# Half of the gate and value weights narrowed inside batch 0, one projection unit per block

## The chip, the cores and the metric

One core of a Trainium2 chip runs the whole program. The metric is the device time of one execution in microseconds (us). TensorE does the matmuls (PE; its weight loads are PEld), VectorE is DVE, ScalarE is ACT, GpSimd is POOL, and SyncE (SP) issues the transfers. Each engine runs its own instructions in the order in which they were put into its queue, and waits on semaphores for the other engines.

## The reference

```
p_packed = attention(p, k, v)              # 8 batches x 8 heads, 32 packed rows, 576 keys, width 64
x = attention(q, p_packed, p_packed)       # 8 x 8 heads, 576 queries against the 32 packed rows
x = x.transpose(0, 2, 1, 3).reshape(4608, 512)
xn = x / sqrt(mean(x*x) + 1e-6) * rms_g
x = (silu(xn @ w_gate) * (xn @ w_val)) @ w_out     # 512 -> 1536 -> 512
h = x @ w_in                                       # 512 -> 2048
out = (h * cos(h)) @ w_out2                        # 2048 -> 512
```

q, k, v, p and rms_g arrive as 32-bit floats. The five weight matrices arrive as 64-bit floats; the kernel makes 32-bit floats of them on the chip, which it calls narrowing.

## The kernel before

**Arithmetic.** A 32-bit product is made of three matmuls of fp32r operands (`mm3`, L143): each operand is split into a high part (ACT, L106) and the rest, the low part, a subtraction (DVE or POOL, L107). `hilo` (L105) does both; its argument `eng` chooses the engine of the low part.

**Narrowing** (`narrow`, L122). A chunk of 128 partitions x 512 numbers (512 KB of doubles) takes five steps, each waiting for the one before: an absolute value on ACT (L129), a maximum with a tiny number (L130, on POOL or DVE), a shift (L133), and two merges (L136, L139) on DVE. `w_gate` and `w_val` make 24 chunks (their tiles are `wraw`, narrowed into `wy`), `w_out` 12 (narrowed into `ny`, then split into `wohl`).

**Packed attention stage** (L489 to L523). 16 steps, two a batch: load keys (`kn`), values (`vn`) and `p`, transpose the keys, form scores (their maximum is L381, once a step), exponentials, and the packed rows. Steps 3 to 15 also load and narrow the 24 chunks and the first four of `w_out`, 28 in all, by `w_due` (L482), and from step 3 on do the first 26 pieces of the query attention of batch 0 (`attend`, L209). In this stage the order on each engine is chosen by a planner of the framework.

**Projection** (`project`, L555). Everything from L718 on stands in the order in which the code emits it. Instead of multiplying x by the gate and value weights, the kernel multiplies the packed rows by them once, and applies the attention weights to the product. There are 24 units; unit n needs chunk n. A unit splits the chunk of the next unit (`pj_stack`, L546: two high parts on ACT, one low part on DVE and one on POOL, tiles `stk`), does 16 matmuls, copies four PSUM tiles (`mps`) out into two `ev` tiles (two copies on ACT, two on DVE), and sends them to DRAM by six transfers (`m0raw` four, `m` two). There are four `ev` tiles. `pj_to` (L708) runs units up to a number: eight before batch 0, then two in each of its blocks 0 to 7, one ahead of the block's matmuls and one behind.

**Blocks** (L774 on). A batch is 24 blocks, of two halves of the tokens and 12 slices of 128 of the hidden width. Block i does `gv_block` (12 matmuls, `gv`; a sigmoid on ACT L655, two products on DVE, L656 and L657, tile `silu`), a piece of the next batch's query attention (`att_step`), `split_s` (L660: high part on ACT, low part on DVE, tile `shl`), and `acc_block` of block i-2 (12 matmuls, `acc`). gv, the projection and the attention share four PSUM tiles (`ps_gv`). Behind that come the jobs of the table at L772 to L836: load, narrow and split a slice of `w_out` (`WO_AT`: load at, narrow at, split one block later), split the gate and value product of a coming pair of slices (`wm_split`, `SPLIT0`), load a product of batch 1 (`M0_AT`), reload partial sums (`X1_AT`). In batch 0 the low parts of `wm_split` are on DVE (`WM0_POOL`), in the other batches on POOL. `after_project` (L697) frees the projection's memory and opens the pools of the later loads; until then `w_out` slices are loaded into `ev` tiles (slices 4 and 5).

Of the kernel before, what the change touches and what calls it, by code (L numbers as in the profile page):

```python
# [9 lines left out]
F32 = mybir.dt.float32  # L10
# [10 lines left out]
def kernel(  # L21
# [22 lines left out]
    HALF = S // 2  # L44
# [3 lines left out]
    NCK = FF1 // 256  # L48
# [14 lines left out]
    WRAW_B = 3  # L63
    WO_U = 4
    SEG, M0_D = 6, 0
    W_FROM, W_TO, W_POOL = 3, 16, 3
    ATT_U, U_ATT, U_ATT_N = 26, 3, 2
    PJ_0, PJ_F, PJ_L = 8, 2, 0
    STT_M, STT_P = 4, 0
    STK_M, STK_P, STK_B, EV_B = 1, 3, 2, 4  # L70
    EV_DVE = (1, 3, 5, 7)
    WM0_POOL = False
    W2_I0, W2_AT, W2_POOL = 25, (1, 3, 5, 7, 14, 18), False
    T_END, F3_B = 2, 3
    LAG, LAG_B = 2, 3
    WO_AT = {4: (0, 2), 5: (2, 4), 6: (7, 9), 7: (8, 10), 8: (9, 11), 9: (10, 12), 10: (12, 14), 11: (13, 16)}
    M0_AT, M_AT = (9, 10, 11, 12, 13, 14), (3, 5, 7, 9, 11, 14)
    ATT_ORD = "t00 t01 x00 x01 x02 x03 t10 r00 t11 s00 x10 x11 p00 x12 p01 x13 - r10 - s10 - p10 p11"
    ATT_ORD0 = "t00 t01 x00 x01 x02 x03 r00 s00 p00 p01 t10 t11 x10 x11 x12 x13 r10 s10 p10 p11"
    AL_AT = 16  # L80
    X1_AT = (14, 20)
    ATT_FROM, ATT_TO, ATT_FROM0, N_ATT = 0, 48, 0, 43
    WM_O, M_I0 = 0, 11
    BX, BS, BW = 0, 3, 6
# [24 lines left out]
    def load_w(pool, tag, src, bufs=None):  # L109
        r, f = src.shape  # L110
        j = r // 128
        shape = [128, j, f, 2] if wide else [128, j, f]
        t = pool.tile(shape, I32 if wide else F32, tag=tag, name=tag, bufs=bufs)
        if wide:
            nc.sync.dma_start(
                out=t.rearrange("p j f t -> p j (f t)"), in_=src.bitcast(I32).rearrange("(j p) f -> p j f", p=128)
            )
        else:
            nc.sync.dma_start(out=t, in_=src.rearrange("(j p) f -> p j f", p=128))
        return t  # L120

    def narrow(raw, y, pool=True):  # L122

        if not wide:
            nc.vector.tensor_copy(y, raw)
            return
        yi = y.bitcast(I32)
        up, low = raw[:, :, :, 1], raw[:, :, :, 0]
        nc.scalar.activation(out=y, in_=raw.bitcast(F32)[:, :, :, 1], func=AF.Abs)  # L129
        (nc.gpsimd if pool else nc.vector).tensor_scalar(  # L130
            out=y, in0=y, scalar1=TINY_HI, scalar2=None, op0=ALU.max
        )
        nc.vector.tensor_scalar(  # L133
            out=yi, in0=yi, scalar1=3, scalar2=0x3FFFFFFF, op0=ALU.logical_shift_left, op1=ALU.bitwise_and
        )
        nc.vector.scalar_tensor_tensor(  # L136
            out=yi, in0=up, scalar=-0x40000000, in1=yi, op0=ALU.bitwise_and, op1=ALU.bitwise_or
        )
        nc.vector.scalar_tensor_tensor(  # L139
            out=yi, in0=low, scalar=29, in1=yi, op0=ALU.logical_shift_right, op1=ALU.bitwise_or  # L140
        )
# [296 lines left out]
    w_y = {}  # L438

    def w_load(n):  # L440
        if n >= 4 * NCK:
            wo_load(n - 4 * NCK, u3, "wraw")
            return
        i, a = divmod(n, 2)
        c, gv = divmod(i, 2)
        w = w_val if gv else w_gate
        w_raw[n] = load_w(u3, "wraw", w[a * 256:(a + 1) * 256, c * 256:(c + 1) * 256], WRAW_B)

    def w_prep(n):
        if n >= 4 * NCK:  # L450
            wo_prep(n - 4 * NCK, u3)
            return
        i, a = divmod(n, 2)
        c, gv = divmod(i, 2)
        if a == 0:
            w_y[i] = wm_p.tile([128, 4, 256], F32, tag="wm", name="wy")
        narrow(w_raw.pop(n), w_y[i][:, 2 * a:2 * a + 2], n % W_POOL == W_POOL - 1)

    att_done = [0]
    late = {}  # L460
# [4 lines left out]
    def wo_load(f, pool, tag):  # L465
        wo_raw[f] = load_w(pool, tag, w_out[f * 128:(f + 1) * 128, :], {"wraw": WRAW_B, "ev": EV_B}.get(tag))

    def wo_prep(f, pool):
        y = pool.tile([128, 1, DM], F32, tag="ny", name="ny", bufs=2 if "w2" in late else 1)
        narrow(wo_raw.pop(f), y, False)  # L470
        wo_y[f] = y
        if f < WO_U:
            wo_split(f)
# [3 lines left out]
        o = wo_t[f] = wo_p[f >= WO_U].tile([128, 2, DM], F32R, tag="wo", name="wohl")  # L477
        hilo(y[:, 0], o[:, 0], o[:, 1], nc.gpsimd if f >= WO_U else None)

    n_w = 4 * NCK + WO_U  # L480

    def w_due(i):  # L482
        a, b = (n_w * max(0, min(x, W_TO) - W_FROM) // (W_TO - W_FROM) for x in (i, i + 1))
# [180 lines left out]
    def acc_block(b, hf, f):  # L664
        n = NF1 if b else SEG
        if f % n == 0:
            acc_t[b, hf] = [ps_acc.tile([128, HALF], F32, tag="acc", name="acc") for _ in range(KD)]
        sh = s_t.pop((b, hf, f))
        wo = wo_t[f]
        for d in range(KD):  # L670
            mm3(
                acc_t[b, hf][d], wo[:, 0, d * 128:(d + 1) * 128], wo[:, 1, d * 128:(d + 1) * 128],
                sh[:, 0], sh[:, 1], f % n == 0, f % n == n - 1,
            )
        if f % n == n - 1:
            c0 = b * S + hf * HALF
            for d2 in range(2):
                x1_at = x1_dram[:, 2 * d2:2 * d2 + 2, c0:c0 + HALF]
                x1 = x1_t.pop((b, hf, d2), None)
                if x1 is None:  # L680
                    x1 = late.get("x", f1).tile([128, 2, HALF], F32, tag="x1", name="x1")
                if f >= n:
                    for r in range(2):
                        nc.vector.tensor_tensor(out=x1[:, r], in0=acc_t[b, hf][2 * d2 + r], in1=x1[:, r], op=ALU.add)
                else:
                    nc.vector.tensor_copy(x1[:, 0], acc_t[b, hf][2 * d2])
                    nc.scalar.activation(out=x1[:, 1], in_=acc_t[b, hf][2 * d2 + 1], func=AF.Copy)  # L687
                nc.sync.dma_start(out=x1_at, in_=x1)

    x1_t = {}  # L690

    def x1_load(hf):
        for d2 in range(2):
# [75 lines left out]

    wm_next = [(b, c) for b in range(1, B) for c in range(NCK)] + [("w", x) for x in range(NCK)]  # L770
    B1 = 2 * NF1
    SPLIT0 = (-1, 1, 3, 5, 7, 9, 13, 14, 16, 19, 21, 23)  # L772
    wm_split()
    for i in range(len(seq) + LAG):  # L774
        b, hf, f = seq[min(i, len(seq) - 1)]
        j = i % B1
        if i < len(seq):
            if j == 0:
                if att is not None:
                    for _ in att:  # L780
                        pass
                att = attend(b + 1) if b + 1 < B else None
                att_done[0] = 0
                if b == B - 1:
                    ast.close()
                    rst.close()
                    bx["p"] = ctx.enter_context(tc.tile_pool(name="bx", bufs=2, side="right", reuse_waits="tile"))
            if b == 0:
                pj_to(PJ_0 + PJ_F * i + 1)
            t = gv_block(b, hf, f)  # L790
            att_step(2 * i)
            split_s(b, hf, f, t)
            if b == 0:
                pj_to(PJ_0 + PJ_F * (i + 1))
                if pj_n[0] == 4 * NCK and not late:
                    after_project()
        if i >= LAG:
            acc_block(*seq[i - LAG])
            att_step(2 * i + 1)
            b, hf, f = seq[i - LAG]  # L800
            if (b, hf) == (B - 1, 0):
                if f == BX:
                    load_x(0)
                if f in (BS, BS + 2):
                    split_x(0, (f - BS) // 2)
                if f >= BW and f < BW + 4:
                    w2_split(f - BW + NF1)
                if f >= BW - 2 and f < BW + 2:
                    w2_load(f - BW + 2 + NF1)
                if f >= NF1 - 2:  # L810
                    w2_load(f - NF1 + 2)
            if (b, hf) == (B - 1, 1):
                w2_split(f)
                if f + 2 < NF1:
                    w2_load(f + 2)
            b, hf, f = seq[min(i, len(seq) - 1)]
        for n, (at, to) in WO_AT.items():
            if at == i:
                wo_load(n, *((late["w2"], "raw") if late else (pr_p, "ev")))
            if to == i:  # L820
                wo_prep(n, late.get("w2", f1))
            if to + 1 == i:
                wo_split(n)
        if i in X1_AT:
            x1_load(X1_AT.index(i))
        if j == AL_AT and b < B - 2:
            att_load(b + 2)
        if i in SPLIT0 if i <= SPLIT0[-1] else b < B - 1 and hf == 1 and f % 2 == 1:
            wm_split()
        if i < len(seq) and b == B - 1 and j >= 11 and j % 2:  # L830
            if j < 23:
                wm_load(wm_next.pop(0))
            if j > 11:
                wm_split()
        if b < B - 1 and j in (M_AT if b else M0_AT):
            wm_load(wm_next.pop(0))  # L836
        if i >= W2_I0 and j in W2_AT:
            w2_fetch()
            w2_narrow(len(w2_items) > 0)
# [112 lines left out]
```

## Time and profile before

| what | value |
|---|---|
| median of 3 runs | 1806.87 us (1806.51 to 1807.89) |
| profiled execution | 1800.86 us |
| its span, first to last instruction | 1799.1 us |
| PE busy | 1701.4 us, 95% of the span |
| DVE busy | 1151.8 us, 64% |
| ACT busy | 921.0 us, 51% |
| POOL busy | 216.0 us, 12% |
| mean granted clock of TensorE | 0.983 |

Busy times are those of the profiled execution, and its own time is 1800.86 us, 1.76 us more than the span. The median of the runs without a profile is 6.0 us above it. A share of the whole span says little here, since the stages differ: the packed attention stage lies from 0 to about 172 us, eight projection units to 215.67 us, batch 0 (its first gv matmul to that of batch 1) from 215.67 to 382.18 us, batch 1 from 382.18 to 472.70 us. The granted clock is the share of TensorE's full clock; it has two levels, 1.2 and 2.4 GHz, so a value between is a mean of both.

### The profile page before, as it was taken

How to read it: one execution, taken by the hardware profiler on the slowest of the kernel's cores; microseconds unless marked ns; L12 is line 12 of the kernel's file. 1: busy time of each engine (PE TensorE's matmuls, PEld its weight loads, DVE VectorE, ACT ScalarE, POOL GpSimd, SP SyncE). 2: the span in 40 equal slices, each digit the busy share in tenths (PEclk: the TensorE clock that was granted, in tenths of full speed). 3: DMA queues.
4: the chain of work that ended last, by engine and by line, in shares of the span. 5: the costliest groups of instructions: out<-in, count | busy, mean ns of one | idle time of the engine just before them, and what ended most of it. 6: DMA issues, size and time to landing. Idle time of an engine off the chain costs nothing.

```text
span 1799.1 us, 26917 instructions
## 1 busy us (share of the span) xinstructions
PE 1701.4 (95%) x10144; PEld 1526.2 (85%) x10144; DVE 1151.8 (64%) x2212; ACT 921.0 (51%) x1773; POOL 216.0 (12%) x186
## 2 busy tenths in 40 slices
PE   7878678799999999999999999999999999999998
PEld 5766568699999999999999788888888888888887
DVE  4677567867676767676756756565656566555554
ACT  4767556445444444454444645454545555454444
POOL 2111222321212121212121300000000000000000
PEclk9989889899999999999999999999999999999999
DMA  9993677434343424242213301010101010100000
GB/s 253 250 255 112 199 210 221 142 108 133 98 135 96 137 94 139 92 143 90 90 61 113 125 1 48 0 48 0 48 0 48 1 47 15 33 1 24 1 24 24
DMA packets 117802, 164.55 MB, mean 91 GB/s; under 512 B 26792, under 2 KB 82088, under 8 KB 117672
## 3 DMA queue, kind: packets, MB, share of 16 engines
q1 hardware_dynamic: 117672, 162.83, 30.7%
q8 instruction: 79, 1.29, 0.3%
q14 instruction: 51, 0.42, 0.1%
HBM read 107.61 MB, written 52.04 MB: 89 GB/s over the span
## 4 chain that ended last, share of the span: by engine, by line
PE 77%; DVE 5%; ACT 3%; DMA 2%; issue 1%; SPq 1%; POOL 0%; DVEq 0%; ACTq 0%
PE ops L146 7%; PE ops L144 7%; PE ops L145 7%; PE hp L144 7%; PE hp L145 7%; PE hp L146 7%; PE gv L144 5%; PE acc L144 5%; PE acc L145 5%; PE acc L146 5%; PE gv L145 5%; PE gv L146 5%; PE sp L227 1%; DMA m<-ev 1%; PE qtp L217 1%
## 5 line engine op out<-in xcount | busy, mean ns | idle before, releaser
L144 PE MATMUL gv<-apt,wmhl 128*128 128x288 f32 x768 | 235.5, 307 | 34.2 <-DVE silu L656 20.1
L144 PE MATMUL acc<-shl,wohl 128*128 128x288 f32 x768 | 234.5, 305 | 0.3 <-ACT x L687 0.3
L144 PE MATMUL hp<-xhl,wmhl 128*128 128x512 f32 x576 | 225.0, 391 | 4.2 <-DVE r L872 4.2
L145 PE MATMUL acc<-shl,wohl 128*128 128x288 f32 x768 | 228.7, 298 | 0.0
L146 PE MATMUL acc<-shl,wohl 128*128 128x288 f32 x768 | 228.6, 298 | 0.0
L145 PE MATMUL gv<-apt,wmhl 128*128 128x288 f32 x768 | 228.0, 297 | 0.0
L146 PE MATMUL gv<-apt,wmhl 128*128 128x288 f32 x768 | 227.4, 296 | 0.0
L145 PE MATMUL hp<-xhl,wmhl 128*128 128x512 f32 x576 | 224.7, 390 | 0.0
L146 PE MATMUL hp<-xhl,wmhl 128*128 128x512 f32 x576 | 224.6, 390 | 0.0
L144 PE MATMUL ops<-w2hl,ghl 128*128 128x512 f32 x576 | 224.2, 389 | 0.0
L145 PE MATMUL ops<-w2hl,ghl 128*128 128x512 f32 x576 | 224.1, 389 | 0.0
L146 PE MATMUL ops<-w2hl,ghl 128*128 128x512 f32 x576 | 223.0, 389 | 0.0
L872 DVE TENSOR_TENSOR r<-r,hp 128x512 f32<-128x512 f32 x144 | 99.0, 687 | 188.7 <-ACT r L871 188.7
L870 ACT ACTIVATE r<-r 128x512 f32<-128x512 f32 x144 | 91.1, 632 | 250.2 <-DVE r L869 248.5
L106 ACT ACTIVATE shl<-silu 128x288 fp32r<-128x288 f32 x192 | 85.2, 444 | 236.2 <-DVE silu L657 234.7
L107 POOL TENSOR_TENSOR wmhl<-wmraw,wmhl 128x512 fp32r<-128x512 f32 x100 | 129.4, 1315 | 520.2 <-ACT wmhl L106 507.3
L144 PEld LDWEIGHTS gv<-apt,wmhl 128*128 128x128 f32 x768 | 145.4, 189 | 38.9 <-DVE silu L656 22.6
L865 ACT ACTIVATE kk<-hp,magic 128x512 f32<-128x512 f32 x144 | 99.3, 690 | 126.0 <-PE hp L146 126.0
L144 PEld LDWEIGHTS acc<-shl,wohl 128*128 128x128 f32 x768 | 145.6, 190 | 0.6 <-ACT x L687 0.5
L145 PEld LDWEIGHTS gv<-apt,wmhl 128*128 128x128 f32 x768 | 145.9, 190 | 0.0
L145 PEld LDWEIGHTS acc<-shl,wohl 128*128 128x128 f32 x768 | 145.9, 190 | 0.0
L146 PEld LDWEIGHTS gv<-apt,wmhl 128*128 128x128 f32 x768 | 145.6, 190 | 0.0
(138 smaller groups left out, 3435.2 us busy)
## 6 DMA issues: line engine op xcount, KB each, us to landing
wmraw<-m SPq DMA_DIRECT2D x42, 512.0 KB
m<-ev SPq DMA_DIRECT2D x24, 512.0 KB
raw<-in_moe_w_out_dram SPq DMA_DIRECT2D x22, 512.0 KB
x_dram<-x SPq DMA_DIRECT2D x36, 288.0 KB
kn<-in_k_dram SPq DMA_DIRECT2D x16, 576.0 KB
vn<-in_v_dram SPq DMA_DIRECT2D x16, 576.0 KB
qnat<-in_q_dram SPq DMA_DIRECT2D x32, 288.0 KB
m<-ev SPq DMA_DIRECT2D x24, 384.0 KB
```

What stands on the lines that cost most here:

```text
L106: nc.scalar.activation(out=hi, in_=src, func=AF.Copy)
L107: (eng or nc.vector).tensor_tensor(out=lo, in0=src, in1=hi.bitcast(F32), op=ALU.subtract)
L144: nc.tensor.matmul(ps, lhi, rhi, start=first, stop=False)
L145: nc.tensor.matmul(ps, lhi, rlo, start=False, stop=False)
L146: nc.tensor.matmul(ps, llo, rhi, start=False, stop=last)
L217: nc.tensor.transpose(tp[:, c * CP:(c + 1) * CP], qv[:, i, 2 * c:2 * c + 2, :].rearrange("p c d -> p (c d)"), ident[:CP, :CP],)
L227: nc.tensor.matmul(sp[:, i, 2 * c:2 * c + 2, :], qT[:, i, c * CP:(c + 1) * CP], bq[:, 2 * j + i], start=True, stop=True,)
L865: nc.scalar.activation(out=kk, in_=hp, func=AF.Identity, scale=1.0 / TWO_PI, bias=magic[:, 0:1])
L870: nc.scalar.activation(out=r, in_=r, func=AF.Abs)
L872: nc.vector.tensor_tensor(out=r, in0=r, in1=hp, op=ALU.mult)
```

## The change

Chunks 12 to 23 of gate and value leave the packed attention stage (`W_KV = 12`). Chunks 12 and 13, and slice 4 of `w_out`, are loaded just before block 0; block i (0 to 11) narrows chunk 12 + i behind its `acc_block`, with the maximum on POOL, and issues the load of chunk 14 + i. Their buffers are those that later hold the split slices of `w_out`. The 16 projection units of batch 0 are spread: two in blocks 0 and 1, one in blocks 2 to 13. Both low parts of `pj_stack` go to POOL (`STT_P = 4`), those of `wm_split` in batch 0 too. The tables move: the pools of the later loads open in block 14, the loads for batch 1 start in block 14, slices 10 and 11 of `w_out` have one block between load and narrowing. The order inside the packed attention stage is still the planner's.

```diff
     W_FROM, W_TO, W_POOL = 3, 16, 3
+    W_KV = 12
-    PJ_0, PJ_F, PJ_L = 8, 2, 0
-    STT_M, STT_P = 4, 0
+    PJ_0, PJ_L, LATE_AT = 8, 0, 14
+    PJ_AT = [9, 10, 11, 12] + [min(24, 12 + x // 2) for x in range(1, 45)]
+    STT_M, STT_P = 4, 4
-    WM0_POOL = False
+    WM0_POOL = True
-    WO_AT = {4: (0, 2), 5: (2, 4), 6: (7, 9), 7: (8, 10), 8: (9, 11), 9: (10, 12), 10: (12, 14), 11: (13, 16)}
-    M0_AT, M_AT = (9, 10, 11, 12, 13, 14), (3, 5, 7, 9, 11, 14)
+    WO_AT = {4: (-1, 1), 5: (1, 3), 6: (8, 10), 7: (10, 12), 8: (11, 13), 9: (12, 14), 10: (14, 15), 11: (15, 16)}
+    M0_AT, M_AT = (14, 15, 16, 17, 18, 20), (3, 5, 7, 9, 11, 14)
-    X1_AT = (14, 20)
+    X1_AT = (15, 21)
...
     def w_load(n):
-        if n >= 4 * NCK:
-            wo_load(n - 4 * NCK, u3, "wraw")
+        if n >= W_KV:
+            wo_load(n - W_KV, u3, "wraw")
             return
+        wy_load(n, u3, "wraw", WRAW_B)
+
+    def wy_load(n, pool, tag, bufs=None):
...
-        narrow(w_raw.pop(n), w_y[i][:, 2 * a:2 * a + 2], n % W_POOL == W_POOL - 1)
+        narrow(w_raw.pop(n), w_y[i][:, 2 * a:2 * a + 2], on_pool)
...
-    n_w = 4 * NCK + WO_U
+    n_w = W_KV + WO_U
...
-                    x1 = late.get("x", f1).tile([128, 2, HALF], F32, tag="x1", name="x1")
+                    x1 = x1_tile(b == 0, d2)
...
+    def x1_tile(first, d2):
+        if first:
+            return (wo_p[1], f1)[d2].tile([128, 2, HALF], F32, tag=("wo", "x1")[d2], name="x1")
+        return late["x"].tile([128, 2, HALF], F32, tag="x1", name="x1")
...
-    SPLIT0 = (-1, 1, 3, 5, 7, 9, 13, 14, 16, 19, 21, 23)
+    SPLIT0 = (-1, 1, 3, 9, 11, 15, 17, 18, 19, 20, 22, 23)
     wm_split()
+    wy_load(W_KV, wo_p[1], "wo")
+    wy_load(W_KV + 1, wo_p[1], "wo")
+    wo_load(WO_U, wo_p[1], "wo")
...
             if b == 0:
-                pj_to(PJ_0 + PJ_F * i + 1)
+                pj_to(PJ_AT[2 * i])
             t = gv_block(b, hf, f)
             att_step(2 * i)
             split_s(b, hf, f, t)
             if b == 0:
-                pj_to(PJ_0 + PJ_F * (i + 1))
-                if pj_n[0] == 4 * NCK and not late:
+                pj_to(PJ_AT[2 * i + 1])
+                if i == LATE_AT:
                     after_project()
...
+        n = W_KV + i
+        if n < 4 * NCK:
+            wy_prep(n, True)
+            if n + 2 < 4 * NCK:
+                wy_load(n + 2, wo_p[1], "wo")
         for n, (at, to) in WO_AT.items():
             if at == i:
-                wo_load(n, *((late["w2"], "raw") if late else (pr_p, "ev")))
+                wo_load(n, *((late["w2"], "raw") if late else (wo_p[1], "wo")))
```

## Rows read from the trace of the kernel before

**Rows 1.** Stretches in us, with each engine's busy us (instructions), clock, DMA share, GB/s
```profile
core 0: us, PE busy (x) PEld busy (x) DVE busy (x) ACT busy (x) POOL busy (x), PEclk, DMA share, GB/s
8.00:152.00 144.00, 121.12 (x665) 96.54 (x664) 99.80 (x258) 92.93 (x226) 26.90 (x24) 0.94 1.00 255
172.00:215.67 43.67, 29.09 (x181) 25.66 (x180) 23.69 (x42) 25.15 (x48) 10.24 (x9) 0.84 0.67 195
215.67:382.18 166.51, 130.37 (x924) 124.85 (x925) 119.84 (x207) 88.88 (x178) 45.04 (x35) 0.93 0.58 173
382.18:472.70 90.52, 89.88 (x710) 89.65 (x709) 63.37 (x138) 42.94 (x97) 17.29 (x14) 1.00 0.36 113
```

**Rows 2.** DMA of the first 172 us: all of it, and the gate chunks
```profile
DMA packets 32526, 38.22 MB, mean 222 GB/s; under 512 B 10496, under 2 KB 25856, under 8 KB 32512
...
wraw<-in_moe_w_gate_dram SPq DMA_DIRECT2D x12, 512.0 KB
```

**Rows 3.** Steps of the packed stage, each from one score maximum to the next
```profile
61.20:74.60 13.40, 12.74 (x91) 10.80 (x90) 9.52 (x26) 9.32 (x24) 2.28 (x3) 1.00 0.94 264
...
143.90:151.20 7.30, 6.91 (x46) 5.69 (x45) 6.08 (x19) 5.03 (x14) 1.00 (x1) 1.00 0.74 239
151.20:160.20 9.00, 7.30 (x45) 5.71 (x43) 8.13 (x18) 8.03 (x19) 1.91 (x2) 1.00 0.04 12
sum 142.50, PE 120.42 PEld 96.44 DVE 106.67 ACT 97.90 POOL 27.99; mean PE 8.03 PEld 6.43 DVE 7.11 ACT 6.53 POOL 1.87
```

**Rows 4.** Batch 0 in parts: blocks 2 to 6, 7 to 13, 14 to 23
```profile
239.67:295.66 55.99, 46.06 (x346) 44.31 (x347) 43.64 (x65) 34.49 (x65) 17.16 (x13) 0.94 0.69 205
295.66:335.36 39.70, 30.43 (x207) 29.43 (x205) 28.51 (x55) 19.51 (x40) 3.70 (x3) 0.87 0.62 188
335.36:382.18 46.82, 38.69 (x282) 37.75 (x281) 35.57 (x69) 20.92 (x49) 18.99 (x16) 0.96 0.36 116
```

**Rows 5.** Waits (us in total, times, longest), blocks 2 to 6, then 7 to 23
```profile
PE gv L144 <- ACT ev L574: 11.3, 7, 3.3
...
PE gv L144 <- DVE silu L656: 16.8, 5, 8.4
```

**Rows 6.** Chain of waits from block 10's silu to block 11's: start us, us, what
```profile
320.23 0.37 DVE silu L656
...
322.44 0.57 ACT ny L129
...
324.18 0.44 DVE ny L133
...
324.64 0.70 DVE ny L136
...
325.36 0.69 DVE ny L139
326.06 0.37 DVE silu L656
...
326.52 0.47 DVE silu L657
```

**Rows 7.** Timeline of block 0: a unit's two high parts and two copies on ACT
```profile
219.26 1.27 ACT L106 ACTIVATE stk<-wy 64x512 fp32r<-64x512 f32 x2
...
220.55 1.09 ACT L574 ACTIVATE ev<-mps 128x512 f32<-128x512 f32 x2
```

**Rows 8.** Groups on POOL to 383 us: shapes, count | busy us, mean ns | idle before
```profile
L107 POOL TENSOR_TENSOR stk<-wy,stk 64x512 fp32r<-64x512 f32 x24 | 32.2, 1344 | 102.2 <-DVE stk L107 40.8 <-ACT stk L106 31.4 <-PE mps L570 14.0
...
L130 POOL TENSOR_SCALAR wy<-wy 128x512 f32<-128x512 f32 x8 | 12.2, 1530 | 57.0 <-ACT wy L129 39.0 <-DMA wraw<-in_moe_w_gate_dram 11.3 <-PE pp L409 6.7
```

**Rows 9.** Timeline of block 14: a shift on DVE beside low parts on POOL
```profile
345.17 3.41 DVE L133 TENSOR_SCALAR ny<-ny 128x512 int32<-128x512 int32 x1
...
345.82 2.48 POOL L107 TENSOR_TENSOR wmhl<-wmraw,wmhl 128x512 fp32r<-128x512 f32 x2
```

**Rows 10.** Start of block 3, PE alone, just behind a wait of 3.3 us
```profile
251.83:255.00 3.17, 3.17 (x14) 0.50 0.76 235
```

More of the change, by code (lines that the diff above doesn't have):

```diff
@@ L446, in w_load, with wy_prep @@
         w = w_val if gv else w_gate
-        w_raw[n] = load_w(u3, "wraw", w[a * 256:(a + 1) * 256, c * 256:(c + 1) * 256], WRAW_B)
+        w_raw[n] = load_w(pool, tag, w[a * 256:(a + 1) * 256, c * 256:(c + 1) * 256], bufs)
     def w_prep(n):
-        if n >= 4 * NCK:
-            wo_prep(n - 4 * NCK, u3)
+        if n >= W_KV:
+            wo_prep(n - W_KV, u3)
             return
+        wy_prep(n, n % W_POOL == W_POOL - 1)
+    def wy_prep(n, on_pool):
         i, a = divmod(n, 2)
```

## The prediction

> **What bounds the kernel now.** I read the busy times by stage first. In batch 1 PE is busy 89.88 of 90.52 us [rows 1]: from there on PE is the bound, and since the change touches nothing behind batch 0, its whole effect is the time at which batch 1 starts (382.18 us). Before that lie three stages with different bounds.
>
> The packed attention stage, 0 to 172 us: between 8 and 152 us the DMA engines are busy 1.00 of the time at 255 GB/s, while PE, DVE and ACT have 121, 100 and 93 of 144 us [rows 1]. The transfers set the pace. The steps show it too: 15 of them take 142.5 us, 9.5 each, up to 13.4; the last two, in which the weight loads thin out and stop, take 7.3 and 9.0 [rows 3].
>
> Eight projection units, 43.67 us: DMA share 0.67, clock 0.84 [rows 1].
>
> Batch 0: 166.51 us against 90.52 of batch 1 [rows 1]. Its blocks 2 to 6 take 11.2 each (55.99 / 5) [rows 4]; PE's waits there are for ACT's copies out of PSUM (11.3 us), which stand behind the ev transfers; later ones, 16.8 us, are for the silu product on DVE [rows 5]. This second kind matters for the change. The chain of waits shows its round: silu, a high part on ACT, the absolute value of a weight slice on ACT, the narrowing steps on DVE, and only then the next silu, because DVE works in order: 326.06 - 320.23 = 5.83 us a round [rows 6].
>
> **Part 1, twelve chunks leave the packed stage.** 12 x 512 KB = 6.29 MB of the 38.22 MB [rows 2]; at 255 GB/s that is 24.7 us, the most that can come back. The least: if the steps were held by their own chain alone, nothing. What is late next: PE is busy 8.03 us a step [rows 3], and the two thin steps average 8.15. The remaining bytes, 31.9 MB, ask for 125 us in place of 150, that is 9.5 x 125 / 150 = 7.9 a step. Two limits this near to each other don't both run full: I take 8.5 us a step, nearest to the thin steps. 15 x (9.5 - 8.5) = **-15 us**, ends 0 and -24.7.
>
> A rule of the Trainium skill speaks against this part. "DMA: Bandwidth & Descriptors", section "Bandwidth", has a transfer of 1 MB at 341 GB/s. By that figure 38.22 MB would take an estimated 112 us of the 172, the transfers would not be the bound, part 1 would be worth near nothing and the sum below would be +18. The trace disagrees: the engines are busy all the time at 255 [rows 1], and I go by that.
>
> **Part 2, units 0 to 7.** Both low parts of a stack on POOL, 2 x 1.34 = 2.7 us in place of two engines side by side [rows 8]; a unit takes some 5 us there (43.67 / 8 = 5.5 with the tail of the attention), and the stack is made one unit ahead. Hidden; I add **+1** for attention's scaling on DVE meeting more POOL work, and for three loads (1.5 MB, 6 us at 255 GB/s) that now stand on SP's queue ahead of block 0's transfers. Ends 0 and +6.
>
> **Part 3, blocks 0 to 13.** This is where the chunks went, and I work out the round as rows 6 has it. In blocks 2 to 11, behind the silu product: high part on ACT 0.42 (an estimate: in the round shown three ACT pieces fill the 1.27 us from the silu's end, 320.23 + 0.37 + 0.47 + 0.10, to the absolute value at 322.44 [rows 6]); two high parts of the next stack 1.27; two ev copies 1.09 [rows 7]; absolute value 0.57 [rows 6]; maximum on POOL 1.53 [rows 8], which is not queued longer, as the two low parts before it (2.7) start 1.1 us behind the silu and end at 3.8, when the absolute value is due to (3.4 to 3.8); shift and merges 0.44 + 0.70 + 0.69; silu 0.37 + 0.47 [rows 6]. Sum 7.55, with a hand-over of some 0.05 at each of four crossings between engines 7.75. Attention's pieces on ACT stand partly in the round: ACT is busy 42.94 us in 24 blocks of batch 1, 1.8 each [rows 1], of which I put 0.4 in. **8.1 us a block.** All links are strict: POOL's maximum waits for ACT, everything on DVE behind the shift waits for POOL, the next silu among it, and ACT's next high part waits for that silu.
>
> PE needs less: 90.52 / 24 = 3.8 for gv, acc and attention [rows 1], and 16 matmuls of a unit at 46.06 / 346 = 0.133 us [rows 4], 2.1, together 5.9. The transfers too: two ev tiles and a chunk, about 1.6 MB in 8.1 us, is 195 GB/s, and an ev tile now has two blocks (16 us) to land, so the wait of rows 5's first line should go. SP has one issue more a block. In exchange, what POOL does behind the maximum locks DVE out: a shift beside two low parts took 3.41 us in place of 0.44 [rows 9]. Block 9 (a split): +2.5. Block 3 (split, and a slice of w_out narrowed: four DVE steps, 0.44 + 0.44 + 0.70 + 0.69 = 2.3): +4.8. Block 10 (a slice): +2.3. Blocks 2 and 4 (one low part): +1.3 each. Block 11 (three low parts): +3.9. Together 16. Blocks 2 to 11: 81 + 16 = 97. Blocks 0 and 1, with two units each, two chunks, a slice and a split: 25, against 24.0 before (239.67 - 215.67). Blocks 12 and 13, a unit and a slice but no chunk: 7 each. Sum 136 against 119.7 (335.36 - 215.67): **+16**, ends -5 (nothing locked out, blocks of 7.6) and +35 (rival b).
>
> Blocks 14 to 23: slices 10 and 11 have one block between load and narrowing; before they had two and three, and still DVE held PE up here (46.82 us against 10 x 3.8 = 38) [rows 4]. In exchange there is one slice less in them. **+1**, ends -5 and +5.
>
> **Sum.** -15 + 1 + 16 + 1 = +3 on the profiled 1800.86 us, 1804; the median of the runs is 6.0 above the profiled execution, so 1806.87 + 3 = **1810 us**. This kernel can't be told from no change within 0.2%, 3.6 us.
>
> **Rivals.**
> (a) The transfers give everything back, and the round in batch 0 is shorter than its sum. For it: DMA share 1.00 over 144 us. Against it: 8.03 us of PE in a step. Price: -24.7 + 1 + 8 + 1 = -14.7, 1792.
> (b) Slower: TensorE's clock falls in blocks 2 to 11. The round leaves PE idle 8.1 - 5.9 = 2.2 us in each. Behind a wait of 3.3 us the granted clock was 0.50, and 14 matmuls took 3.17 us, 0.226 each [rows 10], against 0.133. A block's 44 would take 10 us in place of 5.9, and from a clock that is low a little over half of the time on ((8.1 - 5.9) / (10 - 5.9)) PE would set the pace: (10 - 8.1) x 10 = +19 at worst; I price it at +12: 1822. Against it: in the stage of eight units PE idled a third of the time and still had 0.84 [rows 1]; at 0.84 a block asks for about 7 us, under 8.1.
> By the Trainium skill ("TensorE: Matmul & The Clock Gate", Part 1) the low clock is the default and activity lifts it. By that rule a stage that idles in every block is at risk of the low clock throughout, and the time would be (b)'s worst, 1829; no stretch of this trace as long as ten blocks stays at 0.50.
> (c) The change doesn't do what it says: the steps of the packed stage are held by their own chain (one of 13.4 us had PE busy 12.7 [rows 3]) and give back only 6: +12, 1819.
>
> **Chances.** Forecast 0.45 (its own range 1802 to 1818; of it 0.05 faster, 0.22 same, 0.18 slower), (a) 0.27 (0.25 faster, 0.02 same), (b) 0.18 slower, (c) 0.10 (0.08 slower, 0.02 same). Together faster 0.30, same 0.26, slower 0.44. The range leaves a tenth on each side: 1793, near (a)'s price, to 1825, above (b)'s.
>
> **What would show it.** The score maxima of the packed stage 8.5 us apart, batch 0's first gv matmul near 201 us and batch 1's near 385. Blocks 5 to 8 at 8.1 us each, and in the chain of waits the round ACT absolute value, POOL maximum, DVE shift and merges, silu; PE's wait for the silu product in place of ACT's copies. Block 9 near 10.5, block 3 near 13. I am wrong if DVE's shift doesn't wait for POOL's maximum, if blocks 5 to 8 take under 7 us, or if the packed stage ends more than 20 us sooner.

## The result and the profile after

The changed kernel takes 1827.12 us (median of 4 runs, 1824.31 to 1827.46) against 1806.69 us before on the same chip (4 runs, 1801.41 to 1807.89): ratio 1.0116, 95% interval 1.0093 to 1.014. It is slower by 1.2%. Its profiled execution took 1827.46 us, close to its median; the one of before (1800.86 us) lay 6 us under its own, so the two traces differ by 26.6 us of span where the medians differ by 20.4.

| us, profiled executions | before | after | difference | predicted |
|---|---|---|---|---|
| last transpose of the packed stage | 171.7 | 161.8 | -9.9 | -15 |
| from there to batch 0's first gv matmul | 44.0 | 43.8 | -0.2 | +1 |
| blocks 0 to 13 | 119.7 | 151.4 | +31.7 | +16 |
| blocks 14 to 23 | 46.8 | 50.4 | +3.6 | +1 |
| batch 1 to the end | 1416.9 | 1418.2 | +1.3 | 0 |

The first row is from one trace of each kernel, and the end of that stage differs from trace to trace; over all traces of both orders it is -15.6 (worked out below, under part 1). From here on line numbers are those of the changed kernel: narrowing is L131 (absolute value), L132 (maximum), L135 (shift), L138 and L141 (merges), a high part is L108, a low part L109, a unit's matmuls are L577 and L578, its copies L580 and L582, the sigmoid is L663 and the two products behind it (silu) L664 and L665.

Stretches of the changed kernel, with the columns of [rows 1]: first four stages that answer to [rows 1], then two packed steps ([rows 3]), then blocks 0 to 13, 5 to 7, a piece of block 10, and blocks 14 to 23 ([rows 4]).

```profile
8.00:152.00 144.00, 123.75 (x703) 99.30 (x703) 85.99 (x235) 95.15 (x233) 22.77 (x23) 0.94 0.86 211
161.80:205.62 43.82, 30.93 (x182) 27.70 (x182) 17.41 (x32) 24.83 (x47) 20.71 (x17) 0.81 0.65 191
205.62:407.46 201.84, 148.00 (x926) 139.98 (x926) 128.73 (x217) 95.54 (x190) 97.53 (x73) 0.84 0.58 173
407.46:500.31 92.85, 90.49 (x710) 89.79 (x709) 63.64 (x138) 43.11 (x98) 17.82 (x15) 1.00 0.37 115
...
61.30:76.00 14.70, 13.00 (x91) 11.06 (x91) 9.58 (x25) 9.27 (x23) 2.77 (x3) 1.00 0.92 247
145.00:151.90 6.90, 5.19 (x32) 3.79 (x30) 1.91 (x6) 6.03 (x13) 2.59 (x3) 1.00 0.00 0
...
205.62:357.05 151.43, 106.82 (x646) 100.44 (x646) 92.41 (x150) 73.00 (x138) 73.96 (x54) 0.82 0.61 182
265.52:291.72 26.20, 20.92 (x153) 19.85 (x151) 17.32 (x31) 14.27 (x26) 13.02 (x10) 0.94 0.69 201
317.73:322.70 4.97, 4.97 (x24) 4.95 (x24) 2.89 (x5) 2.67 (x5) 2.54 (x2) 0.52 0.20 67
357.05:407.46 50.41, 41.18 (x283) 39.54 (x282) 36.32 (x68) 22.54 (x52) 23.57 (x19) 0.90 0.52 147
```

The packed stage moved fewer bytes (the total of its DMA, which answers to [rows 2]) and its steps, from the first score maximum at 17.9 us to the last at 151.9, take 8.93 us in place of 9.5; the long step is no shorter (14.7 us, before 13.4).

```profile
DMA packets 29260, 31.91 MB, mean 197 GB/s; under 512 B 10304, under 2 KB 25664, under 8 KB 29248
```

Batch 0 gave all of that back and more. Its waits (us in total, times, longest; from 205 to 380 us), against [rows 5]:

```profile
DVE wy L135 <- POOL wy L132: 38.6, 12, 5.5
...
PE mps L577 <- DVE silu L664: 30.0, 12, 5.0
...
PE gv L146 <- ACT wmhl L108: 9.3, 3, 4.5
...
PE gv L146 <- ACT ev L582: 2.9, 1, 2.9
```

DVE's shift (L135) waits in all 12 chunks for POOL's maximum, and PE's unit waits for the silu product that is queued behind that shift on DVE. The copies out of PSUM, which led before in blocks 2 to 6, are down to one wait.

The chain of waits from 280 to 287 us shows the round at its shortest (the end of silu in block 6 to that in block 7 is 8.2 us). The columns are those of [rows 6].

```profile
280.19 0.63 ACT stk L108
...
280.94 1.29 POOL stk L109
...
282.31 1.00 POOL stk L109
...
283.68 1.50 POOL wy L132
...
285.20 0.44 DVE wy L135
...
285.67 0.70 DVE wy L138
...
286.39 0.69 DVE wy L141
287.08 0.38 DVE silu L664
```

That is the predicted round. The maximum stands behind POOL's two low parts, which end at 283.6, 0.3 us behind ACT's absolute value; the prediction had the two end together. The same chain between blocks 10 and 11 shows what the prediction did not have:

```profile
317.31 0.38 DVE silu L664
...
317.73 0.58 PE mps L577
...
319.81 0.24 PE acc L146
...
322.45 0.22 PE acc L148
322.67 0.26 PE atp L261 x3
...
322.95 0.41 ACT ahl L108
...
323.39 0.68 ACT wy L131
...
324.22 1.50 POOL wy L132
...
325.74 0.44 DVE wy L135
...
327.62 0.35 DVE ny L132
...
329.87 0.38 DVE silu L664
```

From 317.73 to 322.95 the round stands on PE. The absolute value of the next chunk (ACT, L131) is queued behind `ahl`, the high part of attention's second piece; `ahl` waits for PE's transposes `atp`; and these stand behind the second half of the unit and all twelve matmuls of `acc_block`. Two lines of the timeline show both waits:

```profile
317.73 0.58 PE L577 MATMUL mps<-stk,ppT 128*128 128x256 f32 x1 [4.86 <-DVE silu L664]
...
322.95 0.41 ACT L108 ACTIVATE ahl<-atp 128x288 fp32r<-128x288 f32 x1 [1.96 <-PE atp L261]
```

PE had just waited 4.9 us for silu, and its clock in this stretch was 0.52 (1.2 GHz nearly throughout): an acc matmul took 0.24 us where 0.13 is usual. By this trace the round feeds itself, since a wait of PE slows the work that the next silu then waits for; no run tests that by itself.

### The profile page after: what moved, and what is told of

The parts are those of the page before. It is cut to its first block, busy times and chain, and to the rows that moved or that the text cites. A ratio compares the mean times of both kernels' runs of the same rounds, so it can differ in the third digit from the quotient of the medians.

```text
span 1825.7 us, 26951 instructions
## 1 busy us (share of the span) xinstructions
PE 1715.4 (94%) x10144; PEld 1539.9 (84%) x10144; DVE 1129.5 (62%) x2168; ACT 921.4 (50%) x1773; POOL 275.0 (15%) x230
## 4 chain that ended last, share of the span: by engine, by line
PE 77%; DMA 8%; DVE 7%; ACT 4%; POOL 2%; issue 2%; SPq 1%; POOLq 0%; ACTq 0%; DVEq 0%
PE ops L148 7%; PE ops L146 7%; PE ops L147 7%; PE hp L146 7%; PE hp L147 7%; PE hp L148 7%; PE acc L146 5%; PE acc L147 5%; PE acc L148 4%; PE gv L146 4%; PE gv L148 4%; PE gv L147 4%; DMA m<-ev 2%; DMA wmraw<-m 1%; PE pp L411 1%
## 5 line engine op out<-in xcount | busy, mean ns | idle before, releaser
L146 PE MATMUL acc<-shl,wohl 128*128 128x288 f32 x768 | 237.6, 309 | 0.4 <-DVE x L692 0.4
L147 PE MATMUL acc<-shl,wohl 128*128 128x288 f32 x768 | 232.1, 302 | 0.3 <-DVE shl L109 0.3
L148 PE MATMUL acc<-shl,wohl 128*128 128x288 f32 x768 | 231.6, 302 | 0.0
L108 ACT ACTIVATE shl<-silu 128x288 fp32r<-128x288 f32 x192 | 85.2, 444 | 257.8 <-DVE silu L665 256.6
L109 POOL TENSOR_TENSOR wmhl<-wmraw,wmhl 128x512 fp32r<-128x512 f32 x100 | 129.4, 1317 | 513.3 <-ACT wmhl L108 513.3
L146 PEld LDWEIGHTS gv<-apt,wmhl 128*128 128x128 f32 x768 | 146.6, 191 | 22.6 <-ACT wmhl L108 9.9
L148 PEld LDWEIGHTS gv<-apt,wmhl 128*128 128x128 f32 x768 | 146.4, 191 | 4.9 <-POOL wmhl L109 4.9
L147 PEld LDWEIGHTS acc<-shl,wohl 128*128 128x128 f32 x768 | 149.0, 194 | 0.5 <-DVE shl L109 0.5
L146 PEld LDWEIGHTS acc<-shl,wohl 128*128 128x128 f32 x768 | 148.9, 194 | 0.5 <-DVE x L692 0.5
L148 PEld LDWEIGHTS acc<-shl,wohl 128*128 128x128 f32 x768 | 148.3, 193 | 0.0
```

Of the source, the lines that this page charges most:

```text
L108: nc.scalar.activation(out=hi, in_=src, func=AF.Copy)
L109: (eng or nc.vector).tensor_tensor(out=lo, in0=src, in1=hi.bitcast(F32), op=ALU.subtract)
L146: nc.tensor.matmul(ps, lhi, rhi, start=first, stop=False)
L147: nc.tensor.matmul(ps, lhi, rlo, start=False, stop=False)
L148: nc.tensor.matmul(ps, llo, rhi, start=False, stop=last)
```

## The experiments

Runs sent together shared the runs of the kernel before. "Batch 0" is from its first gv matmul to that of batch 1 in the profile, 201.8 us in the changed kernel. Each edit is against the changed kernel. The first theory was that the in-order round of [rows 6], with POOL's maximum as its slowest link, holds batch 0; its rival, that DVE is slowed or locked out by POOL's low parts beside it. The later ones ask what makes the round longer than its sum, and why the packed stage ends where it does.

**The maximum on DVE.**

```diff
-            wy_prep(n, True)
+            wy_prep(n, False)
```

> The changed kernel with one thing different: in blocks 0 to 11 the maximum of a chunk (1.5 us on POOL) is on DVE (0.43 us). Theory 1, the in-order round: everything on DVE behind the shift waits for POOL's maximum, and the next silu with it. Then DVE's wait for POOL (38.6 us over 12 blocks) is gone, each of 12 rounds is about 1.2 us shorter, batch 0 takes 187 in place of 201.8 us, the time is near 1813. Theory 2, the lock: low parts on POOL keep DVE's two-input steps out, whatever the maximum does; then batch 0 stays within 4 us of 201.8 and the time between 1823 and 1831.

Measured: 1805.31 us (10 runs; before 1806.17), ratio 0.9994, interval 0.9977 to 1.001; batch 0 181.5 us, blocks 0 to 13 131.4. The whole loss in time goes with one link of the round, though DVE has more to do (batch 0 itself stays 15 us above the 166.5 of before, which the shorter packed stage pays for). Its stretch and its wait:

```profile
203.60:385.20 181.60, 140.20 (x927) 132.79 (x926) 134.90 (x229) 95.30 (x190) 80.51 (x61) 0.88 0.64 193
...
DVE wy L132 <- ACT wy L131: 15.7, 9, 3.0
```

38.6 us of waiting for POOL became 15.7 for ACT. The order of the round is confirmed, and the low parts, which stayed on POOL, do not hold batch 0 by themselves. The link was worth 20.3 us where 15 were expected and 12 x (1.49 - 0.43) = 13 lie in the maximum itself; where the rest comes from is not shown.

**The three steps on DVE one block later**, ahead of the second unit call of the next block, so that DVE never waits for the maximum in front of a silu.

`narrow_rest` holds the shift and the two merges.

```diff
+        if not later:
+            narrow_rest(raw, y)
+
+    def narrow_rest(raw, y):
...
             split_s(b, hf, f, t)
+            if w_rest:
+                narrow_rest(*w_rest.pop(0))
             if b == 0:
                 pj_to(PJ_AT[2 * i + 1])
```

> The changed kernel with the same work, but DVE's three steps of a chunk (shift, two merges) stand one block later, behind split_s and ahead of the projection, so that POOL's maximum has half a block to end before DVE comes to it. Theory 1, the in-order round: DVE no longer sits behind POOL; rounds of blocks 5 to 9 fall from 8.9 to 6.5 to 7 us, batch 0 to 170 to 180, the time to 1797 to 1807. Theory 2, the lock and the amount of work on POOL and DVE: the same work meets the same ports, batch 0 stays above 195, the time above 1820.

Measured: 1812.8 us (8 runs), ratio 1.0041, interval 1.002 to 1.0062; batch 0 191.4 us, between what the two theories gave. DVE's wait for POOL is gone, but the stack's high part (ACT) now waits for the third step (L145 in this kernel), and the sigmoid (L671), on the same ACT, behind it:

```profile
ACT stk L108 <- DVE wy L145: 35.1, 12, 4.4
...
DVE silu L672 <- ACT silu L671: 28.2, 13, 4.3
```

Less than half of the expected gain came, and the rest turned into this new wait; a block of delay moved the round to ACT and did not open it.

**All chunks back in the packed stage**, the rest of the change kept.

```diff
-    W_KV = 12
+    W_KV = 24
...
-    wy_load(W_KV, wo_p[1], "wo")
-    wy_load(W_KV + 1, wo_p[1], "wo")
```

> The changed kernel with all 24 chunks back in the packed attention stage; one projection unit a block, the low parts on POOL and the moved tables stay. Theory 1: the packed stage ends 10 us later again (last tp matmul near 172 in place of 162), and batch 0, whose rounds lose absolute value, maximum, shift and merges (3.9 us each), is bound by PE in most blocks: 160 to 168 us, the time 1795 to 1805. Theory 2, the low parts on POOL are what costs: batch 0 stays above 180, the time above 1815.

Measured: 1796.01 us (6 runs), ratio 0.9947, interval 0.9929 to 0.9965; batch 0 159.8 us. Against the changed kernel the start of batch 0 moved back by 12.2 us (217.8) and batch 0 lost 42.0. Its batch 0, with the columns of [rows 1]:

```profile
217.77:377.56 159.79, 131.79 (x927) 124.96 (x925) 107.01 (x181) 88.86 (x179) 79.58 (x61) 0.93 0.61 180
```

Without the chunks, one unit a block, the low parts on POOL and the moved tables are together a gain; the chunks are the loss.

**The low parts back on DVE.**

```diff
-    STT_M, STT_P = 4, 4
+    STT_M, STT_P = 4, 0
...
-    WM0_POOL = True
+    WM0_POOL = False
```

> The changed kernel with the low parts where they were before: one of the two of a stack on DVE, and those of batch 0's splits on DVE. Theory 1, the in-order round: the maximum no longer queues behind a second low part (0.4 us a block), and nothing stands behind it on POOL in the split blocks, but DVE has 0.7 us more a unit and 1.4 a split in its own queue ahead of the silu; batch 0 changes by -8 to +4 us, the time is 1819 to 1831. Theory 2, the lock: batch 0 falls by 15 or more, the time to 1812 or less.

Measured: 1824.46 us (4 runs), ratio 1.0107, interval 1.0082 to 1.0132; batch 0 199.8 us. POOL has a third less work in batch 0 (63.5 us, was 97.5) and the time stays, so the lock as the cause of the loss falls; DVE got 6 us more work in exchange, so a small share of it is not excluded. The shift's longest is still 1491 ns (minimum, median, maximum):

```profile
L135 DVE TENSOR_SCALAR wy<-wy x12: 412/428/1491, 217.1 to 340.0; 128x512 int32<-128x512 int32 x12
```

**Five splits one block sooner.**

```diff
-    SPLIT0 = (-1, 1, 3, 9, 11, 15, 17, 18, 19, 20, 22, 23)
+    SPLIT0 = (-1, 0, 2, 8, 10, 14, 17, 18, 19, 20, 22, 23)
```

> The changed kernel with five splits of batch 0's gate and value products one block sooner (blocks 0, 2, 8, 10, 14 in place of 1, 3, 9, 11, 15). The trace of the changed kernel has PE waiting 13.0 us for split parts, in blocks 2, 4 and 16, where the block needs in its first matmul what was split at the end of the block before. Theory 1, the in-order round on DVE and ACT sets the pace of blocks 2 to 13, PE's wait there is beside it: only block 16's part comes back, 3 to 6 us, the time is 1821 to 1825. Rival, just-in-time splits are a cost of their own: all 13 us come back, 1813 to 1816.

Measured: 1818.01 us (4 runs; before 1806.37), ratio 1.0073, interval 1.0051 to 1.0094. The time lies between the two forecasts. Batch 0 is 197.2 us, 4.6 less: the size that the theory expected, but not in block 16 alone, as it had it, since blocks 0 to 13 gave 3.6 and blocks 14 to 23 gave 1.1 (these two parts differ by 0.9 and 1.5 us between the two traces of the changed kernel, so the shares are rough). The other 5 us of the gain are in the packed stage, which this edit does not touch: it ended at 156.5 us. That is taken up below.

**Attention's second piece ahead of `acc_block` in batch 0**, the edit that takes PE out of the round.

```diff
+            if i < B1:
+                att_step(2 * i + 1)
             acc_block(*seq[i - LAG])
-            att_step(2 * i + 1)
+            if i >= B1:
+                att_step(2 * i + 1)
```

> The changed kernel with the second piece of query attention of a block of batch 0 ahead of acc_block in place of behind it. The rounds measured 8.9 us in blocks 5 to 9 against 8.1 of the forecast, and 10.6 to 14.4 later against 10.4 to 12. Theory A: the piece's ACT copy stands ahead of the chunk's absolute value on ACT, and waits for PE transposes that stand behind 12 acc matmuls, so PE's project and acc matmuls are in the round; ahead of acc they are not: batch 0 falls by 6 to 12 us, the time to 1815 to 1821. Rival B: it is the low clock of TensorE alone, which stretches all of PE's work: within 4 us of the changed kernel, 1823 to 1831.

Measured: 1813.3 us (10 runs), ratio 1.004, interval 1.0023 to 1.0056; batch 0 189.8 us, 12.0 less. A timeline of the round from block 10 to 11 (ACT, POOL, DVE; start, us, engine, line):

```profile
308.19 1.09 ACT L582 ACTIVATE ev<-mps 128x512 f32<-128x512 f32 x2
309.19 0.41 ACT L108 ACTIVATE ahl<-atp 128x288 fp32r<-128x288 f32 x1
309.62 0.69 ACT L131 ACTIVATE wy<-wo 128x512 f32<-128x512 f32 x1
...
310.47 1.49 POOL L132 TENSOR_SCALAR wy<-wy 128x512 f32<-128x512 f32 x1 [0.20 <-ACT wy L131]
...
311.99 0.43 DVE L135 TENSOR_SCALAR wy<-wy 128x512 int32<-128x512 int32 x1 [1.90 <-POOL wy L132]
```

`ahl` follows the copies at once, where it waited 1.96 us in the changed kernel, and this round is 10.5 us in place of 12.6. It can follow them because PE's transposes no longer stand behind acc. The granted clock of the blocks hardly moved (0.84 over 205 to 330 us, 0.83 in the changed kernel), so the gain is the order's, not a clock that came back.

**One raw buffer for the chunks of the packed stage in place of three**, to spread their transfers.

```diff
-    WRAW_B = 3
+    WRAW_B = 1
```

> The changed kernel with one buffer in place of three for the raw chunks of the packed attention stage, by which its planner puts one chunk into each step; with three it puts the 12 chunks into the first nine steps, and the last six have none. Theory U1: the first eight steps stayed as loaded as before (58 us against 57), which is why only 10 of the 15 us came back; spread out, the last tp matmul comes at 153 to 157 in place of 161.8, the time is 1818 to 1823. Rival U2: the steps are held by their own chain and ACT's waits for a load with one buffer add to it: last tp at 161 or later, the time 1826 or more.

Measured: 1831.91 us (4 runs), ratio 1.0149, interval 1.0132 to 1.0166; the packed stage ended at 164.3 us, batch 0 began at 214.0. The stage did not end sooner, as the idea had it that bunched transfers in the first half hold it; and from its end to batch 0 it took 49.7 us where the changed kernel took 43.8; there its loss lies, and no run explains it.

**What the runs point to**: the chunks in the packed stage, splits and slices of w_out sooner.

```diff
-    W_KV = 12
+    W_KV = 24
...
-    WO_AT = {4: (-1, 1), 5: (1, 3), 6: (8, 10), 7: (10, 12), 8: (11, 13), 9: (12, 14), 10: (14, 15), 11: (15, 16)}
+    WO_AT = {4: (-1, 1), 5: (1, 3), 6: (3, 5), 7: (5, 7), 8: (7, 9), 9: (9, 11), 10: (14, 16), 11: (15, 17)}
...
-    SPLIT0 = (-1, 1, 3, 9, 11, 15, 17, 18, 19, 20, 22, 23)
+    SPLIT0 = (-1, 0, 2, 8, 10, 14, 17, 18, 19, 20, 22, 23)
...
-    wy_load(W_KV, wo_p[1], "wo")
-    wy_load(W_KV + 1, wo_p[1], "wo")
```

> All 24 chunks in the packed attention stage (the kernel that measured 1796), with the five splits one block sooner, and slices 6 to 9 of w_out narrowed in blocks 5, 7, 9 and 11, slices 10 and 11 with two blocks between load and narrowing. By the in-order round, the rounds of that kernel at blocks 14 to 17 (9.1, 6.3, 8.0 and 8.0 us, each with a slice to narrow) lose two or three slices to blocks that have room, and PE's 11 us of waits for split parts go: batch 0 takes 148 to 155 in place of 159.8 us, the time is 1785 to 1792. Rival: the rounds only move, as every slice costs its 2.3 us on DVE wherever it stands: within 4 us of 1796.

Measured: 1788.24 us (4 runs), ratio 0.9908, interval 0.9889 to 0.9927; batch 0 151.2 us, as expected. This one beats both kernels.

**The changed kernel again**, no edit.

> The changed kernel itself, a second time, for the size of what differs from run to run in one program. Theory: the packed stage's end is not fixed by the program (in kernels whose packed stage is the same as this one's it lay between 156.5 and 164.7 us), and batch 0 is: blocks 0 to 13 again 149 to 153 us, batch 0 200 to 204 us, the packed stage's last matmul anywhere from 155 to 165. Rival: the end of the packed stage belongs to this program, 161.8 within 1 us again, and the differences between the experiments are effects of their edits.

Measured: 1824.87 us (4 runs; before 1804.71), ratio 1.0099, interval 1.0066 to 1.0132; batch 0 201.2 us, every round from block 4 to 13 within 0.2 us of the first trace; the packed stage ended at 161.8 us again. Blocks 0 to 13 had a clock of 0.79, where the first trace had 0.82:

```profile
206.44:358.75 152.31, 109.21 (x647) 103.31 (x646) 92.44 (x150) 73.18 (x138) 73.88 (x54) 0.79 0.60 180
```

Batch 0 repeats, with a lower clock too. The equal end spoke for the rival, hence the last run below.

**Three edits together**: the maximum on DVE, attention's piece ahead of acc, the splits sooner; the chunks stay in batch 0.

```diff
-            wy_prep(n, True)
+            wy_prep(n, False)
```

(and the diffs of the attention's order and of `SPLIT0` above)

> The changed kernel with three edits, none of which takes a chunk or a unit back: the maximum on DVE, attention's second piece ahead of acc in batch 0, and four splits one or more blocks sooner. Alone they shortened batch 0 by 20.3, 12.0 and 4.6 us. Theory: the round was what held batch 0, and two of the three take links out of the same round, so they don't add in full: batch 0 170 to 178 us, the time 1794 to 1802, below before. Rival (TensorE's low clock holds batch 0 once the round is short; it was 0.82 in the changed kernel's blocks): batch 0 stays at 180 or more, 1804 or above, with the granted clock in it not above 0.85.

Measured: 1796.01 us (8 runs), ratio 0.9948, interval 0.9931 to 0.9964; batch 0 175.0 us.

```profile
203.20:378.10 174.90, 139.45 (x926) 131.71 (x925) 132.97 (x230) 96.82 (x191) 81.55 (x61) 0.89 0.67 200
```

26.8 us of batch 0, where the three alone sum to 36.9: links of one round, as expected. The clock rose from 0.84 to 0.89 with the shorter waits, and the rival, by which the low clock would keep batch 0 at 180 us or more, falls. With the chunks where the change put them the kernel is now faster than before.

**The best version with attention ahead of acc**: the edits of the version with 0.9908 and of the attention's order.

```diff
-    W_KV = 12
+    W_KV = 24
...
+            if i < B1:
+                att_step(2 * i + 1)
             acc_block(*seq[i - LAG])
...
```

> All chunks back in the packed stage, one unit a block, splits and slices of w_out sooner, and attention's second piece ahead of acc in batch 0. Without the last edit: 1788.24, batch 0 151.2 us. Theory: without chunks no POOL link stands in the round, but the slices' narrowing and the next high part on ACT still wait behind attention's piece, which waits behind acc: batch 0 144 to 150, 1782 to 1787. Rival: attention's order matters only where a chunk's narrowing stands behind it; then 150 to 153 and 1787 to 1790.

Measured: 1791.22 us (4 runs), ratio 0.9914, interval 0.9888 to 0.9941; batch 0 150.9 us against 151.2. The rival holds: attention's order matters only while a chunk's narrowing stands behind it. The time is 3 us above that of the version without the edit; in the traces its packed stage, which has the same order, ended at 179.6 us against 174.3.

**Attention ahead of acc, again**, no further edit.

> The kernel with attention's second piece ahead of acc, a second time. Its packed stage issues the same work in the same order as the changed kernel's, yet ended at 154.8 us against 161.8 and 161.8. Theory: each program has its own end for that stage: 154.8 within 1 us again. Rival: the end is drawn anew each time, anywhere from 155 to 165, and the two equal ends of the changed kernel were chance. Batch 0 is 188 to 192 us by both.

Measured: 1814.37 us (8 runs; before 1806.31), ratio 1.0044, interval 1.0024 to 1.0063; batch 0 192.2 us, so that against the two traces of the changed kernel the edit was worth 9.0 to 12.0 us; the packed stage ended at 158.2 us, against 154.8 in the first trace of this program. The theory falls: one program's stage ends 3.4 us apart (on two chips; on a single one, programs with the same order there ended at 157.5 and 159.5). Stretches of the first trace and, in the second fence, of this one:

```profile
8.00:152.00 144.00, 124.07 (x729) 99.95 (x728) 88.81 (x244) 99.26 (x244) 26.14 (x24) 1.00 0.85 213
```

```profile
8.00:152.00 144.00, 126.90 (x718) 101.86 (x716) 87.75 (x241) 97.51 (x239) 26.96 (x24) 0.94 0.83 212
```

The earlier end had the full clock throughout, the later one 0.94.

## Why the prediction was wrong

**The bound** was read rightly: behind batch 0 the time moved by 1.3 us, and the effect is the time at which batch 1 starts, 407.46 us in place of 382.18.

**Part 1** was right, though the two traces show only -9.9 us. Over the nine traces in which twelve chunks are out of the stage and three buffers are kept, its end lies between 154.8 and 164.7 us, on average 159.3. Over the four with all chunks in it (the kernel before and the three experiments with `W_KV = 24`, with the same order in that stage but for the low parts of the first stacks) it lies at 171.7, 174.1, 174.3 and 179.6, on average 174.9. That is 15.6 sooner, with steps of 8.75 us in place of 9.64, and with it the rows of the table sum to +20.8, where the medians have +20.4. Rival (a), all 24.7, fell, and so did (c), 6. With ends that spread over 8 to 10 us in either group, it is luck that forecast and average lie within 1 us. The Trainium skill's figure ("DMA: Bandwidth & Descriptors", section "Bandwidth") of 341 GB/s for 1 MB, by which part 1 would have been worth near nothing, was rightly set aside: the stage got shorter when the chunks left. Whether it was their bytes or their narrowing, which left with them, no run tells apart.

**Part 2** was hidden, as predicted (-0.2 us).

**Part 3 is the step that failed, by its size.** Its mechanism stands: the order of links, the wait of the shift for POOL, PE's wait for silu in place of ACT's copies. The price of 8.1 us holds for the round that has nothing else in it (8.2). But the forecast made +16 of blocks 0 to 13, and it was +31.7. The term that was mis-sized is the line "Attention's pieces on ACT stand partly in the round ... of which I put 0.4 in", and with it "PE needs less". Attention's pieces were counted by how long ACT is busy with them, not by what they wait for. Rounds, from the end of one block's silu product (its second line) to the next:

| us, round ending in block | 3 | 4 | 5 | 6 | 7 | 8 | 9 | 10 | 11 | 12 | 13 | sum |
|---|---|---|---|---|---|---|---|---|---|---|---|---|
| predicted (price of the block before) | 9.4 | 12.9 | 9.4 | 8.1 | 8.1 | 8.1 | 8.1 | 10.6 | 10.4 | 12.0 | 7.0 | 104.1 |
| changed kernel | 10.4 | 15.1 | 9.2 | 9.4 | 8.2 | 10.3 | 9.3 | 10.6 | 12.6 | 14.4 | 9.5 | 119.0 |
| attention ahead of acc | 10.4 | 12.7 | 9.3 | 8.7 | 8.2 | 9.5 | 9.3 | 10.6 | 10.5 | 11.4 | 8.1 | 108.7 |

With the piece ahead of acc, 10.3 of the 14.9 us that were missing are gone (in the second pair of traces 11.5 of 16.2), 2.4, 2.1 and 3.0 of them in rounds 4, 11 and 12; and rounds 4, 10, 11 and 12, in which the prediction had set the lock on DVE and the slices, come out within 0.6 us of it. The 4.6 us that are left are not tested. The trace shows parts of them. In round 9 the maximum stands behind POOL's two low parts, which took 3.8 us where 2.65 is usual, with the piece ahead of acc as well:

```profile
299.41 3.79 POOL L109 TENSOR_TENSOR stk<-wy,stk 64x512 fp32r<-64x512 f32 x2 [3.97 <-DVE sm L250]
```

In round 8 ACT's absolute value is queued behind two copies of acc's sums (L695) and an exponential of attention (L245). The split of the gate and value products just in time is another wait that the prediction did not look for: it priced a split by what it does to DVE, not by who needs it next. Moved sooner it gave 4.6 us of batch 0, but only 1.2 of them in these rounds.

**The lock on DVE** was there. In block 9, beside POOL's low parts, the shift and also the first merge were long (a timeline: DVE, then POOL):

```profile
313.44 1.48 DVE L135 TENSOR_SCALAR wy<-wy 128x512 int32<-128x512 int32 x1 [2.93 <-POOL wy L132]
314.95 1.63 DVE L138 SCALAR_TENSOR_TENSOR wy<-wo,wy 128x512 int32<-128x512 int32 x1
...
313.38 2.66 POOL L109 TENSOR_TENSOR wmhl<-m0raw,wmhl 128x512 fp32r<-128x512 f32 x2
```

1.48 + 1.63 against 0.44 + 0.70: 2.0 us, where 2.5 had been set. As the cause of the whole loss it is ruled out by the run with the low parts on DVE, and by the one that moved the maximum alone.

**Rival (b)** came nearest in time (1822, at worst 1829), and its mechanism, TensorE setting the pace at the low clock, is not what happened. The clock in blocks 5 to 7 was 0.94; in the run that took PE out of the round the blocks gained while their clock stayed; and in the second trace of the changed kernel it was 0.79 over blocks 0 to 13, in place of 0.82, with the same rounds. But the clock had a share that the prediction kept apart: where PE's work stands inside the round it runs at 0.52 behind the wait, 24 matmuls in 4.97 us where 24 x 0.133 = 3.2. The Trainium skill ("TensorE: Matmul & The Clock Gate", Part 1) has the low clock as the default that activity lifts. The traces agree in that the four longest waits of PE in batch 0 (4.0 to 5.0 us) were each followed by a clock of 0.50 over the next 3 us. The low clock throughout, which the prediction saw as the risk of that rule, did not come: 0.82 over blocks 0 to 13.

**Blocks 14 to 23** lost 3.6 us where 1 was set, inside its ends; block 16 alone waited 5.5 us for a split.

## What to carry to other kernels

When work is put into a stage in which every engine runs in order, write down for each instruction ahead of it in its queue not how long it takes but what it waits for, and follow that to the next engine: here an ACT step of 0.41 us carried half a unit and twelve matmuls of TensorE into the round. A new chain through three engines is cheap only if no link of it stands between an engine's result and the next block's start; moving one link (the maximum, 0.43 us on DVE against 1.49 on POOL and two crossings) was worth 20 us over twelve blocks. And test the halves of a change apart: here one half was worth 0.5% and the other cost more than that.

## What the runs showed of the hardware that was not expected

The same packed-stage program ended at 154.8 and at 158.2 us, with a granted clock of 1.00 and 0.94. Between programs whose edits lie behind that stage, the ends reach from 154.8 to 164.7 us, and they go roughly with the clock between 8 and 152 us: 157.5 us at 0.98, 161.8 twice at 0.94, 164.7 at 0.93, the others (156.5 to 159.5) at 0.94 to 0.96. Which of the two follows the other no run shows. How much of it is drawn anew in each execution and how much belongs to the program or the chip is not settled either, so a difference of up to 10 us in this stage between two single traces should not be put down to an edit. Batch 0 itself is told apart better: in blocks 4 to 13 the rounds of the changed kernel repeat within 0.2 us and those with attention ahead of acc within 0.7, and all of batch 0 within 0.6 and 2.4 us.
